# Row loads with six tokens per partition, loads on two queues, a 64-column local mask and a new opening list, in a sparse-attention and gated-MLP kernel

## The chip, the cores and the metric

The kernel runs on one core of a Trainium2 chip. TensorE (PE) multiplies; VectorE (DVE), ScalarE (ACT) and GpSimd (POOL) do the elementwise work; SyncE (SP) only issues transfers (DMAs), and ACT issues some too. The metric is the device time of one execution in microseconds.

## The reference

Eight batches, eight heads, 576 tokens, 64 values per head, all in float32. Heads 0 to 3 see the last 32 tokens (local), heads 4 to 7 see every 32nd token before them (strided). The result, with heads side by side (512 wide), goes through a gated MLP whose gate mixes tokens.

```python
scores = scale * np.matmul(q, k.transpose(0, 1, 3, 2))
rel = pos[:, None] - pos[None, :]
mask_local = (rel >= 0) & (rel < 32)
mask_strided = (rel >= 0) & (pos[None, :] % 32 == pos[:, None] % 32)
attn = softmax(where(mask, scores, -1e9)); x = attn @ v     # heads h < 4 local, others strided

h = gelu_tanh(x @ w_in)                  # w_in 512 x 1024
u, v = h[..., :512], h[..., 512:]
v_n = (v - mean(v)) / sqrt(var(v) + 1e-6) * g_ln
v_s = einsum('ts,bsd->btd', w_sg, v_n) + b_sg[None, :, None]    # 576 x 576 over tokens
return x + (u * v_s) @ w_out             # w_out 512 x 512
```

The weights w_in and w_out arrive as 64-bit floats and are turned into pairs of float32r values (high and remainder) on the core.

## The kernel before

The work is cut into short *steps*, each a two- or three-letter name with an argument; three lists give the order in which they are emitted: START for batch 0 (with batch 1's attention beside it), CYCLE for batches 1 to 6 and LAST for batch 7. A `-` behind a name means batch 0's own attention, `+` the batch after the next, nothing the next batch (for attention) or the present one (for the MLP). Each engine runs its instructions in the order of the list, so a list sets the order on five engines and on the DMA queues at once. A `^` chooses the other of two ways for that step, such as DVE in place of POOL.

The heads go in pairs `hh` = 0 to 3: 0 and 1 are local, 2 and 3 strided. For each pair and batch:

- `LP` (`qk_rows`, batches 0 and 1) loads q and k with tokens on partitions; `TP` and `TC` (`qk_turn`, `qk_turned`) transpose them on PE and copy them from PSUM with ACT. `LQ` and `TQ` do this for the later batches with loads of 32-token blocks and DVE transposes. `TZ` and `LZ` set zeros, `LV` (`v_load`) loads v.
- `SL` and `SS` are the local and strided scores on PE; `MK`, `MX`, `SB`, `EX`, `SU`, `ML` are the softmax: mask added, maximum, subtraction, exponential, sum, scaling. `SB` and `ML` run on POOL, or on DVE with `^`.
- `PL`, `CL`, `CM` and `PS`, `CS` transpose the probabilities, `VA` (`VX`, `VY`) and `PV`, `PW` multiply with v; `XH` and `XL` split the result into high part and remainder (`xt`), `XR` and `XD` store it to memory for the final addition.

The MLP: `va` to `vd` and `v` (products with the v half of w_in), `g` (gelu), `ls`, `lr`, `lm`, `lh`, `ll` (layer norm; `lr` computes the reciprocal root by a seed and three Newton steps, on POOL or with `^` on DVE), `u` and `ug`, `s` (the mixing over tokens, with w_sg transposed by `wl`, `wt`, `wh`, `wm`), `sm`, `sh`, `sl` (gate and its split), `o`, `o2`, `os`, `od` (the output product, the addition of x, the store), `r` and `rt` (x read back).

The conversion of the 64-bit weights is done once, in sixteen parts (0 to 7 of w_in, v half first; 8 to 15 of w_out): `cl` loads, `ca`, `cc` (DVE) and `cb`, `cd` (ACT) take the bits apart, `ce` adds the low word (DVE, or ACT and POOL with `^`), `cf` multiplies (POOL, or DVE with `^`), `cg` (ACT) writes the high part, `ch` (POOL, or DVE with `^`) the remainder. The buffer `stage` holds five parts of w_in, `ob` two of w_out.

All loads are issued by SP (`sp.dma_start`), the stores by ACT. The local mask `mask_l` is 128 x 8 x 64: eight equal blocks, of which two differ in 32 rows, where the first 32 keys lie before the first token.

Of the kernel before, what the change touches and what calls it, by code (L numbers as in the profile page):

```python
# [8 lines left out]
F32 = mybir.dt.float32  # L9
# [15 lines left out]
mk= cl=:1 cl=:2 wb= wc= wd= ca=:1 cb=:1 cc=:1 TZ-:0 LP-:0 TP-:1 ca=:2 cl=:0 ca=:0 cb=:0 cc=:0  # L25
TP-:0 TC-:0 cb=:2 cc=:2 mp= LP-:1 TP-:2 TC-:2 cd=:1 ce=:1 TC-:1 cl=:3 ca=:3 LZ-:0 cd=:0 LP-:3
TZ-:1 TP-^:3 TC-:3 SL-^:0 ml= LP-:2 we= cb=:3 MK-:4 cc=:3 MX-:4 TP-^:6 SB-:4 SL-:1 MK-:5 TP-:4
cd=:3 ce=:3 cf=^:3 TP-^:5 mr= TP-:7 cl=:8 MX-:5 ca=:8 cf=^:1 ce=^:0 SB-^:5 cd=:2 cf=:0 TC-:6
TC-:7 cg=:3 cl=:9 ca=:9 cb=:8 cc=:8 cg=:0 SS-^:3 MK-:3 TC-:5 ce=^:2 LP:1 EX-:4 SU-:4 LP:0 cb=:9
EX-:5 SU-:5 cc=:9 ML-^:4 TP:2 TC-:4 TZ:1 TP^:0 TC:0 cl=:6 cg=:1 ch=:3 SS-^:2 cf=:2 cd=:9 cg=:2  # L30
PL-:4 ch=^:1 ML-^:5 cd=:8 TC:2 LZ-:1 ce=^:8 TP^:3 TC:3 LV-:0 CL-:4 TP:1 ca=:6 ce=:9 cb=:6 MK-:2
MX-:2 cf=:9 cg=:9 SB-^:2 PL-:5 CL-:5 ch=:9 wl=:1 wt=^:1 wh=:1 MX-:3 SB-:3 ch=:2 ch=:0 cc=:6
EX-:2 VX-:0 XHa-:0 cl=:5 wm=:1 ca=:5 cb=:5 CM-:5 VY-:0 TZ:0 TC:1 SU-:2 cd=:6 XLa-:0 LV-:1 XR-:0
EX-:3 SU-:3 cl=:13 ca=:13 VA-:1 XH-:1 XL-:1 cl=:7 XR-:1 XHb-:0 cb=:13 ca=:7 cf=:8 ce=:6 LP:3
ML-:2 PS-^:2 LV-:2 CS-:2 cc=:13 cb=:7 ML-:3 PS-^:3 CS-:3 cc=:5 cd=:5 cf=^:6 LV-:3 SL^:0 cl=:4
SL^:1 MK:0 MX:0 cd=:13 XD-:0 XD-:1 PV-:3 PW-:3 cc=:7 ca=:4 SB^:0 cb=:4 PV-^:2 PW-:2 cc=:4 va:0
XH-:2 XL-:2 XH-:3 XL-:3 XLb-:0 XR-:2 xt vb:0 vc:0 vd:0 ce=^:13 EX:0 LP:2 cd=:4 g:0 ce=^:4 lg=
va:1 cf=:4 vb:1 XD-:2 ce=:5 SU:0 ML^:0 vc:1 LZ:1 vd:1 XR-:3 XD-:3 cf=^:5 TP^:4 v:2 ls:0 lr:0
lm:0 cd=:7 cg=:4 ce=:7 cf=^:7 cg=:6 ch=:6 g:1 ls:1 TP:7 TC:4 vh wl=:4 wt=:4 TC:7 TP^:6 cf=^:13
TC:6 cg=:7 wl=:0 wt=^:0 lm:1 vl SS:3 wh=:0 wm=:0 wh=:4 cg=:5 TP:5 wl=:2 wt=^:2 TC:5 wm=:4 ch=:4  # L40
MK:3 cl=:15 ch=^:5 cg=:8 ch=:7 ch=^:8 SS:2 MK:2 MX:2 lh:0 u:1 g:2 ug:1 lr:1 lh:1 ll:0 wh=:2 u^:2
ls:2 ca=:15 cb=:15 cc=:15 cl=:10 ca=:10 ll:1 lm:2 wm=:2 wl=:3 wt=^:3 wh=:3 TZ+:0 wo= wm=:3
# [59 lines left out]
def tile_sparse_attention_moe(  # L102
# [63 lines left out]
    mask_l = cpool.tile([P, 8, 64], F32, name="mask_l")  # L166
# [10 lines left out]
    def local_mask():  # L177

        pool.memset(mask_l, 0.0)
        for g in range(4):  # L180
            r = slice(32 * g, 32 * g + 32)
            pool.affine_select(
                out=mask_l[r], in_=mask_l[r], pattern=[[0, 8], [1, 64]],
                compare_op=ALU.is_gt, fill=NEG, base=0, channel_multiplier=-1,
            )
            pool.affine_select(
                out=mask_l[r], in_=mask_l[r], pattern=[[0, 8], [-1, 64]],
                compare_op=ALU.is_ge, fill=NEG, base=32, channel_multiplier=1,
            )

        for g, blk in ((0, 1), (1, 5)):
            pool.memset(mask_l[32 * g : 32 * g + 32, blk, 0:32], NEG)
# [158 lines left out]
    def sg_load(t):  # L351
        n = P if t < KF else TL
        wsg_st[t] = p2.tile([P, S], F32, tag="gt", name=f"wsg_{t}")
        sp.dma_start(wsg_st[t][:n], w_sg[t * P : t * P + n, :])
# [52 lines left out]
    def qk_load(b, hh):  # L407

        for nm, src in (("q", q), ("k", k)):
            raw = p1.tile([P, NB, 32], F32, tag="raw", name=f"raw{nm}_{b}_{hh}", bufs=4)  # L410
            for hp in range(2):
                for dh in range(2):
                    qd = 32 * (2 * hp + dh)
                    sp.dma_start(
                        raw[qd : qd + 32],
                        src[b, 2 * hh + hp, :, 32 * dh : 32 * dh + 32].rearrange(
                            "(n t) d -> t n d", t=32
                        ),
                    )
            state[b, hh, "raw" + nm] = raw  # L420
# [19 lines left out]

    def qk_rows(b, hh):

        for nm, src in (("q", q), ("k", k)):
            raw = p1.tile([P, KF + 1, 2, D], F32, tag="raw", name=f"row{nm}_{b}_{hh}", bufs=4)
            for hp in range(2):
                rows = src[b, 2 * hh + hp]
                sp.dma_start(
                    raw[:, 0:KF, hp], rows[0 : KF * P].rearrange("(c p) d -> p c d", p=P)
                )
                sp.dma_start(raw[:TL, KF, hp], rows[KF * P : S])  # L450
            state[b, hh, "row" + nm] = raw
# [12 lines left out]

    def qk_turned(b, x):
        hh, nm = x // 2, "qk"[x % 2]
# [6 lines left out]
        src = state[b, hh, "turn" + nm][:, 0:S]  # L473
        if hh >= NH // 2:
            dst = dst.rearrange("p (c t) -> p c t", c=NCL)
            src = src.rearrange("p (t c) -> p c t", c=NCL)
        act.copy(dst, src)
# [5 lines left out]
    def v_load(b, hh):  # L483
        if hh < NH // 2:
            vv = state[b, hh, "v"].rearrange("p h (j d) -> p h j d", d=D)
            for hp in range(2):
                src = v[b, 2 * hh + hp]
                sp.dma_start(vv[0:64, hp], src.rearrange("(j p) d -> p j d", p=64))
                sp.dma_start(
                    vv[64:128, hp, 1:NJ, :],  # L490
                    src[32 : S - 32].rearrange("(j p) d -> p j d", p=64),
                )
                sp.dma_start(vv[96:128, hp, 0, :], src[0:32])
        else:
            vt = state[b, hh, "v"] = p2.tile([P, 2, NJ * D], F32, tag="v", name=f"v_{b}_{hh}")
            for hp in range(2):
                src = v[b, 2 * hh + hp].rearrange("(p n r) d -> n p (r d)", n=2, r=8)
                for n in range(2):
                    sp.dma_start(vt[TP * n : TP * n + TP, hp, 0 : 8 * D], src[n])
# [30 lines left out]
    def strided_scores(b, hh):  # L530
        qT, kT = state[b, hh, "q"], state[b, hh, "k"]
        ps = state[b, "s", hh] = at_tile(f"ss_{b}_{hh}")
        for rb in range(8):
            for n in range(2):
                c = 8 * n + rb
                for hp in range(2):
# [3 lines left out]
                        qT[hr, c * TP : c * TP + TP],  # L540
                        kT[hr, c * TP : c * TP + TP],
# [6 lines left out]
    def sm_mask(b, x):  # L548

        if x in PARTS:  # L550
# [3 lines left out]
            for a in range(2):  # L554
                if x != 5 - a:
                    m = mask_l[:, 4 * a : 4 * a + 4].rearrange("p a b -> p (a b)")
                    dve.tensor_tensor(
                        sm[:, 512 * a : 512 * a + 512].rearrange("p (h w) -> p h w", h=2),
                        ps[:, :, 256 * a : 256 * a + 256],
                        m[:, None, :].to_broadcast([P, 2, 256]), op=ALU.add,  # L560
                    )
            if x != 4:
                pr = state[b, "sr"]
                dve.tensor_tensor(
                    sm[:, 1024:1152], pr[:, 0, 0:128],
                    mask_l[:, 2:4].rearrange("p a b -> p (a b)"), op=ALU.add,
# [241 lines left out]
    def ln_rsqrt(b, i):  # L808
# [235 lines left out]
```

## Time and profile before

| | |
|---|---|
| Median of 3 runs | 591.0 us (590.96 to 591.58) |
| Profiled execution, its own time | 590.0 us |
| Span from first to last instruction | 588.0 us |
| Mean granted TensorE clock | 0.991 |
| PE, busy | 550.4 us (94%) |
| DVE, busy | 398.1 us (68%) |
| ACT, busy | 270.5 us (46%) |
| POOL, busy | 199.7 us (34%) |
| Data moved by DMA | 69.95 MB, 119 GB/s over the span |

Shares are of the span. PE's busy time counts the matrix products; the weight loads that overlap them stand apart as PEld. A stretch's DMA share is the mean busy share of the 16 DMA engines. Issuing a DMA isn't counted as busy time, on SP or on ACT; it shows as a row of that engine's queue (SPq, ACTq). All steps are recorded in one helper, so every row has the same line number, and tiles tell them apart: `stage` and `cv` belong to the conversion, `rowq` and `rowk` to the row loads, `turnq` and `turnk` to their transposes, `sa`/`sr` and `ss` to local and strided scores, `sml` and `sms` to their softmax.

### The profile page before, as it was taken

How to read it: one execution, taken by the hardware profiler on the slowest of the kernel's cores; microseconds unless marked ns; L12 is line 12 of the kernel's file. 1: busy time of each engine (PE TensorE's matmuls, PEld its weight loads, DVE VectorE, ACT ScalarE, POOL GpSimd, SP SyncE). 2: the span in 40 equal slices, each digit the busy share in tenths (PEclk: the TensorE clock that was granted, in tenths of full speed). 3: DMA queues.
4: the chain of work that ended last, by engine and by line, in shares of the span. 5: the costliest groups of instructions: out<-in, count | busy, mean ns of one | idle time of the engine just before them, and what ended most of it. 6: DMA issues, size and time to landing. Idle time of an engine off the chain costs nothing.

```text
span 588.0 us, 15066 instructions
## 1 busy us (share of the span) xinstructions
PE 550.4 (94%) x6113; PEld 489.9 (83%) x6113; DVE 398.1 (68%) x665; ACT 270.5 (46%) x397; POOL 199.7 (34%) x471
## 2 busy tenths in 40 slices
PE   1766899999999999999999999999999999999996
PEld 1555678888999889988998889988998889988995
DVE  2879997776884577756775577756875588545532
ACT  2486575741573327542572328442572338433320
POOL 6334187240542027220642026310732035302310
PEclk9996999999999999999999999999999999999999
DMA  6778764477842689248832678248831781056002
GB/s 185 178 175 195 151 166 86 104 170 172 181 66 57 146 165 164 41 102 162 168 63 59 159 142 160 42 113 166 169 61 53 166 168 37 1 118 156 1 2 89
DMA packets 262630, 69.95 MB, mean 119 GB/s; under 512 B 248289, under 2 KB 248289, under 8 KB 262562
## 3 DMA queue, kind: packets, MB, share of 16 engines
q1 hardware_dynamic: 181538, 50.12, 39.4%
q10 hardware_dynamic: 81024, 18.89, 15.8%
q8 instruction: 48, 0.79, 0.6%
q14 instruction: 20, 0.16, 0.1%
HBM read 50.09 MB, written 18.87 MB: 117 GB/s over the span
## 4 chain that ended last, share of the span: by engine, by line
PE 77%; DVE 8%; POOL 4%; DMA 3%; ACT 3%; issue 3%; SPq 1%; ACTq 0%; DVEq 0%; POOLq 0%
PE sg L83 18%; PE o L83 17%; PE v L83 15%; PE u L83 14%; PE os L83 3%; PE ss L83 2%; PE ol L83 2%; POOL nt L83 2%; PE sa L83 2%; PE pts L83 2%; DMA stage<-in_moe_w_in_dram 1%; DMA rowq<-in_q_dram 1%; DVE sr L83 1%; PE ptl L83 1%; SPq L83 1%
## 5 line engine op out<-in xcount | busy, mean ns | idle before, releaser
L83 PE MATMUL sg<-wsh,vg 128*128 128x288 f32 x512 | 112.8, 296 | 0.0
L83 PE MATMUL u<-xt,wih 128*128 128x288 f32 x512 | 103.5, 297 | 1.1 <-ACT u L83 1.0
L83 PE MATMUL o<-woh,vg 128*128 128x512 f32 x288 | 95.7, 398 | 1.1 <-DVE gt L83 1.1
L83 PEld LDWEIGHTS sg<-wsh,vg 128*128 128x128 f32 x512 | 85.5, 188 | 0.3
L83 PE MATMUL v<-wih,xt 128*128 128x512 f32 x256 | 83.4, 397 | 1.5 <-ACT xt L83 0.9
L83 PEld LDWEIGHTS u<-xt,wih 128*128 128x128 f32 x512 | 82.1, 188 | 2.6 <-ACT u L83 1.8
L83 PE MATMUL u<-xt,wil 128*128 128x288 f32 x256 | 75.6, 295 | 0.4 <-DVE wil L83 0.4
L83 PE MATMUL sg<-wsl,vg 128*128 128x288 f32 x256 | 75.3, 294 | 0.0
L83 ACT ACT_TABLE_LOAD x40 | 51.3, 1283 | 51.5 <-DMA xd<-xs 26.9
L83 PEld LDWEIGHTS o<-woh,vg 128*128 128x128 f32 x288 | 54.1, 188 | 12.5 <-issue 1.3
L83 PEld LDWEIGHTS v<-wih,xt 128*128 128x128 f32 x256 | 48.0, 188 | 13.3 <-ACT xt L83 1.3
L83 PE MATMUL o<-wol,vg 128*128 128x512 f32 x144 | 56.3, 391 | 0.0
L83 DVE TENSOR_TENSOR ob<-o,xn 128x512 f32<-128x512 f32 x32 | 22.0, 691 | 46.5 <-PE o L83 40.7
L83 ACT CAST vg<-gt 128x576 fp32r<-128x576 f32 (+2 forms) x48 | 22.9, 509 | 61.1 <-DVE gt L83 61.1
L83 PE MATMUL v<-wil,xt 128*128 128x512 f32 x128 | 50.1, 391 | 0.0
L83 PEld LDWEIGHTS u<-xt,wil 128*128 128x128 f32 x256 | 48.0, 188 | 0.6 <-DVE wil L83 0.6
L83 PEld LDWEIGHTS sg<-wsl,vg 128*128 128x128 f32 x256 | 48.2, 188 | 0.0
L83 DVE BATCH_NORM_STATS2 bnst<-hv 128x6 f32<-128x512 f32 (+1 forms) x40 | 27.0, 676 | 17.4 <-ACT hv L83 17.4
L83 POOL TENSOR_TENSOR sms<-sms,sr 100x576 f32<-100x576 f32 x14 | 16.2, 1158 | 64.6 <-DVE sr L83 63.4
L83 DVE TENSOR_TENSOR gt<-sg,u 128x576 f32<-128x576 f32 x32 | 23.6, 739 | 21.3 <-PE sg L83 12.5
L83 ACT ACTIVATE u<-u 128x576 f32<-128x576 f32 x32 | 20.9, 652 | 28.6 <-PE u L83 28.4
L83 POOL TENSOR_SCALAR va<-mv 128x2 f32<-128x2 f32 (+1 forms) x23 | 8.3, 363 | 70.1 <-DVE mv L83 68.9
(152 smaller groups left out, 1094.6 us busy)
## 6 DMA issues: line engine op xcount, KB each, us to landing
xd<-xs ACTq DMA_DIRECT2D x128, 72.0 KB
xn<-xd SPq DMA_DIRECT2D x8, 1024.0 KB
out_dram<-ob ACTq DMA_DIRECT2D x32, 256.0 KB
rawq<-in_q_dram SPq DMA_DIRECT2D x96, 72.0 KB
rawk<-in_k_dram SPq DMA_DIRECT2D x96, 72.0 KB
v<-in_v_dram SPq DMA_DIRECT2D x32, 144.0 KB
v<-in_v_dram SPq DMA_DIRECT2D x64, 72.0 KB
stage<-in_moe_w_in_dram SPq DMA_DIRECT2D x8, 512.0 KB
```

The source lines that it names most:

```text
L83: ins = self.tc.keep_in_program_order(op(*args, **kwargs))
```

## The change

- `START` is written anew. It has the same 428 steps as before, in another order, and with `^` on other steps.
- `loads()` stands in for `sp` in `cl`, `wl`, `LP`, `LQ` and `LV`: with `^` the load is issued by ACT. In CYCLE and LAST no load carries `^`.
- `qk_rows` puts six consecutive tokens on each of 96 partitions, one transfer per head and tensor; before, tokens went over 128 partitions in four blocks and a fifth of 64, in two transfers. The six transposes of 96 partitions yield token order `c, t` (token 6t + c), and the copy behind them, in steps, puts the tokens in their natural order, for strided heads too. The strided scores of batches 0 and 1 then read q and k with 16 words between elements; later batches keep theirs class by class.
- `v_load` joins transfers of two heads: 5 instead of 6 for a local pair, 2 instead of 4 for a strided one.
- `mask_l` is 128 x 64 and is broadcast in the addition; the rows before the first token are set by a `memset` on the sum, one for each half of the heads.
- On DVE the Newton step of `lr` is three instructions instead of four.

The first words of the two lists:

```
before: mk= cl=:1 cl=:2 wb= wc= wd= ca=:1 cb=:1 cc=:1 TZ-:0 LP-:0 TP-:1 ca=:2 cl=:0 ca=:0 cb=:0 cc=:0
        TP-:0 TC-:0 cb=:2 cc=:2 mp= LP-:1 TP-:2 TC-:2 cd=:1 ce=:1 TC-:1 cl=:3 ca=:3 LZ-:0 cd=:0 LP-:3 ...
after:  mk= mp= cl=:3 ca=:3 cl=:1 LP-^:3 cb=:3 cc=:3 ca=:1 cb=:1 cl=:0 cc=:1 cd=:1 cd=:3 cl=:2 TZ-:0
        ca=:2 cl=:8 ml= ce=:3 ca=:0 cb=:0 ce=^:1 TP-^:6 TC-:6 cb=:2 TP-^:7 TC-:7 cf=^:1 cg=:1 cc=:2 ...
```

```diff
+    def loads():
+        return act if alt[0] else sp
...
-    mask_l = cpool.tile([P, 8, 64], F32, name="mask_l")
+    mask_l = cpool.tile([P, 64], F32, name="mask_l")
...
-        sp.dma_start(conv[i], halves[i][0])
+        loads().dma_start(conv[i], halves[i][0])
...
+    RP = 96
+    RT = S // RP
...
-            raw = p1.tile([P, KF + 1, 2, D], F32, tag="raw", name=f"row{nm}_{b}_{hh}", bufs=4)
+            raw = p1.tile([P, RT, 2, D], F32, tag="raw", name=f"row{nm}_{b}_{hh}", bufs=4)
             for hp in range(2):
-                rows = src[b, 2 * hh + hp]
-                sp.dma_start(
-                    raw[:, 0:KF, hp], rows[0 : KF * P].rearrange("(c p) d -> p c d", p=P)
+                loads().dma_start(
+                    raw[0:RP, :, hp], src[b, 2 * hh + hp].rearrange("(p c) d -> p c d", c=RT)
                 )
-                sp.dma_start(raw[:TL, KF, hp], rows[KF * P : S])
...
+        for c in range(RT):
             pe.transpose(
-                ps[:, kk * P : kk * P + n],
-                raw[:n, kk].rearrange("p h d -> p (h d)"), ident[:n, :n],
+                ps[:, c // 3, c % 3 * RP : c % 3 * RP + RP],
+                raw[0:RP, c].rearrange("p h d -> p (h d)"), ident[0:RP, 0:RP],
             )
...
-        act.copy(dst, src)
+        act.copy(
+            dst.rearrange("p (t a c) -> p t a c", a=2, c=RT // 2),
+            state[b, hh, "turn" + nm][:, :, 0:SH].rearrange("p a (c t) -> p t a c", t=RP),
+        )
...
-                sp.dma_start(vv[96:128, hp, 0, :], src[0:32])
+            loads().dma_start(vv[96:128, :, 0, :], src[:, 0:32].rearrange("h p d -> p h d"))
...
+            src = v[b, 2 * hh : 2 * hh + 2].rearrange("h (p n r) d -> n p h (r d)", n=2, r=8)
+            for n in range(2):
+                loads().dma_start(vt[TP * n : TP * n + TP, :, 0 : 8 * D], src[n])
...
+        if by_rows(b):
+            qc, kc = (x[:, 0:S].rearrange("p (t c) -> p c t", c=NCL) for x in (qT, kT))
+        else:
+            qc, kc = (x[:, 0:S].rearrange("p (c t) -> p c t", c=NCL) for x in (qT, kT))
...
-                        qT[hr, c * TP : c * TP + TP],
-                        kT[hr, c * TP : c * TP + TP],
+                        qc[hr, c],
+                        kc[hr, c],
...
+                        half.rearrange("p h (g w) -> p h g w", w=64),
+                        ps[:, :, 256 * a : 256 * a + 256].rearrange("p h (g w) -> p h g w", w=64),
+                        mask_l[:, None, None, :].to_broadcast([P, 2, 4, 64]), op=ALU.add,
                     )
+                    dve.memset(half[32 * a : 32 * a + 32, :, 64:96], NEG)
...
+            if eng is dve:
+                dve.scalar_tensor_tensor(t[c], t[c], -0.5, va[c], op0=ALU.mult, op1=ALU.mult)
+                dve.scalar_tensor_tensor(y[c], t[c], 1.5, y[c], op0=ALU.add, op1=ALU.mult)
+                continue
```

More of the change, by code (lines that the diff above doesn't have):

```diff
@@ L31 @@
[L31 to L42, printed above, removed]
@@ new lines @@
+sh:3 cb=:12 ML^:3 LZ:0 cg=:10 cc=:12 VA^:1 cd=:12 LQ+:3 sm:0 ch=:8 cg=:15 cl=:14 ch=^:10 ca=:14
+ch=^:15 ce=^:12 cf=:12 sh:0 sl^:0 TQ+:0 cg=:12 LV:0 sm:1 sh:1 sl:1 r cb=:14 cc=:14 EX:2 LQ+:1
+VA:0 XR:1 PS:3 CS:3 o:0 o^:1 ch=:12 sl:3 cd=:14 ce=:14 cf=^:14 cg=:14 SU:2 ML^:2 XH:0 XL:0
+ch=:14 XH:1 XL:1 LV:3 o^:2 o^:3 o2:2 os:2 XD:1 XR:0 XD:0 o2:0 o2:3 os:3 LV:2 PS^:2 o2:1 PV:3
+PW:3 CS:2 od:2 PV:2 od:3 PW:2 TQ+:1 XH:3 LZ+:1 XL:3 XH:2 XR:3 XD:3 os:1 XR:2 XD:2 od:1 LZ+:0
+os:0 od:0 LV+^:0 LQ+:2 LV+:1 XL:2
@@ L182, in local_mask @@
             pool.affine_select(
-                out=mask_l[r], in_=mask_l[r], pattern=[[0, 8], [1, 64]],
+                out=mask_l[r], in_=mask_l[r], pattern=[[1, 64]],
                 compare_op=ALU.is_gt, fill=NEG, base=0, channel_multiplier=-1,
@@ L186, in local_mask @@
             pool.affine_select(
-                out=mask_l[r], in_=mask_l[r], pattern=[[0, 8], [-1, 64]],
+                out=mask_l[r], in_=mask_l[r], pattern=[[-1, 64]],
                 compare_op=ALU.is_ge, fill=NEG, base=32, channel_multiplier=1,
             )
-        for g, blk in ((0, 1), (1, 5)):
-            pool.memset(mask_l[32 * g : 32 * g + 32, blk, 0:32], NEG)
     mask_s = cpool.tile([P, TP], F32, name="mask_s")
@@ L353, in sg_load @@
         wsg_st[t] = p2.tile([P, S], F32, tag="gt", name=f"wsg_{t}")
-        sp.dma_start(wsg_st[t][:n], w_sg[t * P : t * P + n, :])
+        loads().dma_start(wsg_st[t][:n], w_sg[t * P : t * P + n, :])
     def sg_transpose(t):
@@ L456, in qk_turn @@
         raw = state[b, hh, "row" + nm]
-        ps = state[b, hh, "turn" + nm] = mm_tile(f"turn{nm}_{b}_{hh}").rearrange("p a c -> p (a c)")
-        for kk in range(KF + 1):
-            n = P if kk < KF else TL
+        ps = state[b, hh, "turn" + nm] = mm_tile(f"turn{nm}_{b}_{hh}")
+        for c in range(RT):
             pe.transpose(
-                ps[:, kk * P : kk * P + n],
-                raw[:n, kk].rearrange("p h d -> p (h d)"), ident[:n, :n],
+                ps[:, c // 3, c % 3 * RP : c % 3 * RP + RP],
+                raw[0:RP, c].rearrange("p h d -> p (h d)"), ident[0:RP, 0:RP],
             )
@@ L485, in v_load @@
             vv = state[b, hh, "v"].rearrange("p h (j d) -> p h j d", d=D)
+            src = v[b, 2 * hh : 2 * hh + 2]
             for hp in range(2):
-                src = v[b, 2 * hh + hp]
-                sp.dma_start(vv[0:64, hp], src.rearrange("(j p) d -> p j d", p=64))
-                sp.dma_start(
+                loads().dma_start(vv[0:64, hp], src[hp].rearrange("(j p) d -> p j d", p=64))
+                loads().dma_start(
                     vv[64:128, hp, 1:NJ, :],
-                    src[32 : S - 32].rearrange("(j p) d -> p j d", p=64),
+                    src[hp, 32 : S - 32].rearrange("(j p) d -> p j d", p=64),
                 )
-                sp.dma_start(vv[96:128, hp, 0, :], src[0:32])
+            loads().dma_start(vv[96:128, :, 0, :], src[:, 0:32].rearrange("h p d -> p h d"))
         else:
             vt = state[b, hh, "v"] = p2.tile([P, 2, NJ * D], F32, tag="v", name=f"v_{b}_{hh}")
[L496 to L499, printed above, removed]
+            src = v[b, 2 * hh : 2 * hh + 2].rearrange("h (p n r) d -> n p h (r d)", n=2, r=8)
+            for n in range(2):
+                loads().dma_start(vt[TP * n : TP * n + TP, :, 0 : 8 * D], src[n])
     def blk_pos(hh, hp, j):
@@ L555, in sm_mask @@
                 if x != 5 - a:
[L556 removed]
+                    half = sm[:, 512 * a : 512 * a + 512].rearrange("p (h w) -> p h w", h=2)
                     dve.tensor_tensor(
[L558 to L560 removed]
+                        half.rearrange("p h (g w) -> p h g w", w=64),
+                        ps[:, :, 256 * a : 256 * a + 256].rearrange("p h (g w) -> p h g w", w=64),
+                        mask_l[:, None, None, :].to_broadcast([P, 2, 4, 64]), op=ALU.add,
                     )
+                    dve.memset(half[32 * a : 32 * a + 32, :, 64:96], NEG)
             if x != 4:
@@ L564, in sm_mask @@
                 dve.tensor_tensor(
-                    sm[:, 1024:1152], pr[:, 0, 0:128],
-                    mask_l[:, 2:4].rearrange("p a b -> p (a b)"), op=ALU.add,
+                    sm[:, 1024:1152].rearrange("p (g w) -> p g w", w=64),
+                    pr[:, 0, 0:128].rearrange("p (g w) -> p g w", w=64),
+                    mask_l[:, None, :].to_broadcast([P, 2, 64]), op=ALU.add,
                 )
```

44 lines of the change are left out of this document (24 added, 20 removed).

## The prediction

> **What bounds the kernel now.** I read the busy time of each engine by stretches of the span first, then the chain of work that ended last, then the order of time of the SP queue, and only then single tiles. The columns of the first view are: stretch, its length, busy time (and instructions) of PE, PEld, DVE, ACT and POOL, granted TensorE clock, share of the DMA engines, GB/s.
>
> ```profile
> 0.00:10.00 10.00, 0.00 (x0) 0.00 (x0) 3.41 (x4) 2.87 (x4) 8.53 (x27) 1.00 0.60 164
> 10.00:20.00 10.00, 7.11 (x93) 4.96 (x94) 5.83 (x16) 5.41 (x9) 1.47 (x4) 1.00 0.89 220
> 20.00:30.00 10.00, 7.12 (x92) 5.04 (x92) 7.07 (x14) 2.96 (x6) 4.81 (x8) 1.00 0.65 160
> 30.00:40.00 10.00, 8.21 (x151) 6.86 (x151) 7.36 (x15) 7.91 (x17) 3.78 (x5) 1.00 0.66 155
> 40.00:50.00 10.00, 4.79 (x50) 3.32 (x48) 9.47 (x10) 5.95 (x12) 6.95 (x8) 0.73 1.05 203
> 50.00:62.00 12.00, 9.00 (x255) 7.99 (x257) 11.76 (x27) 7.85 (x14) 2.36 (x3) 0.80 0.82 208
> 62.00:100.00 38.00, 34.38 (x325) 28.61 (x320) 33.01 (x60) 22.87 (x44) 24.39 (x55) 1.00 0.63 135
> 100.00:140.00 40.00, 37.46 (x343) 33.70 (x341) 29.42 (x53) 20.81 (x37) 13.71 (x17) 1.00 0.59 135
> 140.00:584.00 444.00, 442.30 (x4819) 399.46 (x4818) 290.60 (x472) 193.81 (x257) 133.73 (x347) 1.00 0.52 107
> ```
>
> From 140 to 584 us PE idles 1.7 us of 444. From 62 to 140 it idles 6.2 of 78. Before 62 it idles 25.8 of 62. So nearly everything that can be won lies before the first v product, and what follows it is a solid run of PE to the end:
>
> ```profile
> 62.32 0.50 PE L83 MATMUL v<-wih,xt 128*128 128x512 f32 x1
> ...
> 583.50 0.69 DVE ob L83
> ```
>
> The first row is from PE's order of time, the last from the end of the chain: the addition that waits for the last product. From 62.3 to 583.5 are 521.2 us. The products in it are the same after the change, so the time is the moment of the first v product plus that run, corrected for what PE has done ahead of it and for waits behind it.
>
> Ahead of 62 us DVE is the engine that is full, but only late: 21.2 busy of the 22 us from 40 to 62, against 23.7 of the first 40. Why it is short of work there is told by its waits (what waited, for whom: total, times, longest) and by the SP queue:
>
> ```profile
> DVE cv L83 <- DMA stage<-in_moe_w_in_dram: 9.3, 3, 5.1
> DVE cv L83 <- ACT cv L83: 2.2, 2, 1.4
> DVE cx L83 <- DMA cs<-in_moe_w_out_dram: 2.0, 1, 2.0
> ```
>
> ```profile
> 4.29 2.17 SPq L83 DMA_DIRECT2D rowq<-in_q_dram  x4
> 6.50 2.34 SPq L83 DMA_DIRECT2D rowk<-in_k_dram  x4
> 8.88 0.58 SPq L83 DMA_DIRECT2D stage<-in_moe_w_in_dram  x1
> ...
> 33.48 2.28 SPq L83 DMA_DIRECT2D rowk<-in_k_dram  x4
> 35.86 0.53 SPq L83 DMA_DIRECT2D stage<-in_moe_w_in_dram  x1
> 36.43 4.06 SPq L83 DMA_DIRECT2D v<-in_v_dram  x6
> ```
>
> SP issues without a pause: from 4.29 to 36.43 us it sends 48 row loads and five loads of weights, 0.61 us each. DMA engines are at 0.65 to 0.66 of their time from 20 to 40 us, so there the issuing is the limit and not the moving. Of every pair of row loads one carries only 16 KB and costs an issue like the 128 KB one (four in 2.17 to 2.34 us).
>
> **The change, part by part.** *Row loads.* One step LP issues 4 transfers instead of 8, in b = 0 and 1 only; v loads go from 6 to 5 and from 4 to 2. Counting the steps of both lists up to the first v product gives 97 issues before (89 on SP, 8 on ACT) and 60 after (42 on SP, 18 on ACT). At 0.61 us, SP's share of that falls from 54 to 26 us, and 18 issues on ACT take 11 us where 8 took 5. The bytes remain: counted over the lists, 10.6 MB before the first v product and 10.1 after. The DMA engines' share above sums to 48.3 us of full work up to 62 us, so even with free issue the first v product can't come before some 46 us (48.3 x 10.1 / 10.6). That caps the gain of this part at 16 us. What I book is the DVE waits for loads that are not the first one: 9.3 + 2.0 - 5.1 = 6.2 us. DVE's waits for ACT (2.2 in the row above) I leave as they are, since the list has as many such hand-overs as before.
>
> *Six transposes of 96 in place of four of 128 and one of 64.* The columns moved are equal (576).
>
> ```profile
> 10.35 1.41 PE L83 MATMUL turnk<-ident,rowk 128*128 128x128 f32 x5 [10.35 <-DMA rowk<-in_k_dram]
> 78.23 0.86 PE L83 MATMUL turnk<-ident,rowk 128*128 128x128 f32 x5
> L83 PE MATMUL ss<-kT,qT x256: 199/199/273, 30.0 to 85.7; 64*36 64x36 f32 x128
> 81.25 1.31 PE L83 MATMUL ss<-kT,qT 64*36 64x36 f32 x64
> L83 ACT COPY qT<-turnq x8: 617/629/644, 14.2 to 80.2; 128x576 f32<-128x576 f32 x8
> ```
>
> Between no cost and 6/5 of the 1.41 us (0.28 each) or of the later 0.86 us (0.17 each), 16 turns cost 0 to 3.6 us; PE idles around most of them, I book 0.5. The copy behind each turn now reads PSUM in steps; half of the copies in the row above (the strided heads) did so before, and shortest and longest differ by 27 ns, so nothing is booked.
>
> *Strided scores of b = 0 and 1* read q and k from SBUF with 16 words between elements instead of one after the other. No row of this trace has PE reading SBUF so. Bounds: nothing, as for the ACT copies, and a doubling, 1.31 us more for each of four steps (64 matmuls each), 5.2 us, or the 6.7 us of all 256 by their 199 to 273 ns if they overlap as now. I take nothing for the forecast (the copies are the nearest row of a stepped read) and keep the doubling as a rival.
>
> *Local mask.*
>
> ```profile
> L83 POOL TENSOR_SCALAR_AFFINE_SELECT mask_l<-mask_l x8: 648/695/1007, 5.1 to 10.6; 32x512 f32<-32x512 f32 x8
> L83 DVE TENSOR_TENSOR sml<-sa,mask_l x16: 678/688/693, 20.0 to 470.8; 128x512 f32<-128x512 f32 x16
> L83 DVE TENSOR_SCALAR cv<-stage x8: 383/424/879, 5.1 to 63.0; 128x512 int32<-128x512 int32 x8
> L83 POOL TENSOR_SCALAR_AFFINE_SELECT mask_s<-mask_s 36x36 f32<-36x36 f32 x2 | 0.4, 210 | 0.1
> ```
>
> Eight selects of 512 columns become eight of 64, near the 210 ns of the 36-column one: POOL falls from 5.8 to 1.7 us. POOL isn't on the path there, but while it runs them DVE's first field extractions take up to 879 ns instead of 424. I book no gain, as DVE then waited for a load. The mask addition stays at 688 ns, 512 elements either way. Two DVE memsets per batch are new, some 0.2 us each by the nearest small rows (the 210 ns select, the 175 ns in the next fence). Four of the sixteen fall before the first v product (0.8 us, within the list's sum below); the twelve others lie where DVE is busy 290.6 of 444 us, so they cost nothing; without that cover, 2.4 us.
>
> *The list.* Both lists hold the same 428 steps, differently ordered and differently dealt out. POOL gets less; DVE gets the seed-and-Newton step of one v tile (eleven small instructions), two more gate remainders and one more subtraction, and gives up one scaling.
>
> ```profile
> L83 DVE TENSOR_SCALAR sr<-sr 100x16 f32<-100x16 f32 x4 | 0.7, 175 | 0.1
> L83 DVE TENSOR_TENSOR vg<-gt,vg 128x576 fp32r<-128x576 f32 x1 | 0.7, 747 | 0.0
> 32.23 1.52 DVE L83 TENSOR_TENSOR sms<-ss,mask_s 36x576 f32<-36x576 f32 x2 [0.53 <-PE ss L83]
> ...
> 45.70 3.77 DVE L83 TENSOR_SCALAR stage<-stage 128x512 int32<-128x512 int32 x1
> 46.64 2.48 POOL L83 TENSOR_TENSOR wil<-cv,wih 128x512 fp32r<-128x512 f32 x2
> ```
>
> That is 11 x 0.175 + 2 x 0.75, some 3.4 us more DVE over the list. Added up to the step where as much of PE's work is done as at the first sg product before, the list sum on DVE is 82.1 us after against 80.4 before, so I book 1.7 us as a loss. On the other side, head pair 3 comes first. The first weights reach DVE 5.1 us after the start (the longest wait above); its rows are issued right behind them, and two turns of 1.4 us, their copies of 0.6 and the scores of some 2 follow, so that even with 4 us in the queues DVE can mask them by 15 to 16 us. Before, the first strided scores were masked at 32.23. This is work for DVE in just the stretch where it waited, and the reason why I book all 6.2 us. The 3.77 us instruction takes 0.42 elsewhere (the 424 ns row, same shape); it ended within half a microsecond of POOL's work beside it. I price what becomes of it from -3.3 (it does not recur) to +3.3 (one more of it) and take -1.6, half of it away, because POOL has some 10 us less to do in the list.
>
> Sum: -6.2 - 1.6 + 1.7 + 0.5 = -5.6 us. The profiled execution took 590.0 us (span 588.0, 2.0 around it), so it becomes 584.4; the median of the runs shown is 591.0, 1.0 above, so the median becomes 585.4.
>
> **The rivals.** (1) *Deeper.* If DVE really runs full from its first load on, the waits for ACT shrink by half too (1.1), the 3.77 us stall goes whole (1.7 more), and PE does another 2 us of later work ahead of v: 585.4 - 4.8 = 580.6. For it speaks the size of the idle time (17.1 us of DVE before 62); against it that a chain DVE, ACT, DVE, ACT stands behind every half of the weights.
>
> (2) *It changes nothing.* The moving, not the issuing, is the bound: share 1.05 and 0.82 after 40 us, and all bytes still have to come by the first v product. Then what is issued early lands late, the 6.2 us stay, and 591 remains, within a microsecond. Against it: 0.65 and 0.66 from 20 to 40. [...]
>
> (3) *Slower: the second queue blocks ACT.* When ACT and SP issued together the issues took longer, and the activation behind them waited:
>
> ```profile
> 59.67 5.23 ACTq L83 DMA_DIRECT2D xd<-xs  x6
> 61.88 2.28 SPq L83 DMA_DIRECT2D rowq<-in_q_dram  x3
> 64.95 0.72 ACT L83 ACTIVATE cv<-cv,ebias 128x512 int32<-128x512 int32 x1 [5.22 <-DMA xd<-xs]
> ```
>
> 0.87 us each on ACT. Ten issues more there ahead of the first v product cost ACT 8.7 us; behind them in its queue stand the exponent and mantissa steps that DVE waits for. If all of it passes on to DVE: 585.4 + 8.7 = 594.1. It decides from 0.56 us per extra issue passed on in full (5.6 in all). Against it: ACT is busy 32.9 of the first 62 us and can give way.
>
> (4) *Stepped reads slow PE.* Doubled strided scores cost 5.2 us; b = 0's two steps fall where PE idles, b = 1's in the full run, so half of it counts: 588.0. [...]
>
> **How the numbers follow.** Forecast 0.50, deeper 0.20, nothing 0.09, ACT blocked 0.14, stepped reads 0.07. The forecast's own range is 582 to 589. The range for 8 in 10 goes from 578.5, which holds most of the deeper case, to 591.0, which leaves out the blocked queue and half of the unchanged case. A measurement of this kernel can tell 0.2%, 1.2 us: faster is below 589.8 (forecast, deeper and stepped reads, less 0.01 that goes to slower), the same up to 592.2.
>
> **What would show it.** First v product near 56 us instead of 62.3, with the run behind it still 521 us, within 3. DVE's waits for stage loads near 5 us, its first one. SP pausing before 36 us. Transposes of 96 rows at or below 0.3 us apart, strided scores still 1.3 us per 64. The prediction is wrong if the first v product comes early but the gain is given back before 140 us (DVE then is the cause, and its busy time from 62 to 100 would be near 38), if ACT's waits for its own DMA issues rise by 5 us or more, or if PE's time after 140 us changes at all.

## The result and the profile after

The changed kernel takes 581.07 us (median of 5 runs, 580.32 to 583.45) where the kernel before takes 591.58 on the same chip (590.96 to 592.88): ratio 0.9826, interval 0.981 to 0.9842, a gain of 10.5 us. Measured once more beside other kernels on another chip it was 581.43 against 591.89, ratio 0.9829 (0.9802 to 0.9856). Each of the two measurements left a profile: the first was of an execution of 583.45 us, its slowest, the second of one of 580.09. Where they differ I give both.

The moment of the first v product, from PE's order of time, first profile and then second (62.32 before):

```profile
55.70 0.48 PE L83 MATMUL v<-wih,xt 128*128 128x512 f32 x1
```

```profile
54.11 0.48 PE L83 MATMUL v<-wih,xt 128*128 128x512 f32 x1
```

From there to the last product of PE are 521.4 and 519.7 us (521.1 before). So in the first profile the difference to before (590.0 - 583.45 = 6.55) is the shift of the first v product (6.62) and nothing else; in the second (9.9) it is 8.2 of shift and 1.4 behind it.

That the run behind the first v product keeps its length is a sum of changes that nearly cancel. Its first 77.7 us and the rest up to the last product of PE, before and then in the first profile (columns as in the prediction: PE, PEld, DVE, ACT, POOL, granted clock, DMA share, GB/s):

```profile
62.32:140.00 77.68, 71.52 (x656) 62.07 (x653) 62.11 (x111) 43.68 (x80) 38.10 (x71) 1.00 0.61 135
140.00:583.46 443.46, 442.30 (x4819) 399.46 (x4818) 290.10 (x471) 193.81 (x257) 133.73 (x347) 1.00 0.52 107
```

```profile
55.70:133.38 77.68, 75.91 (x839) 67.30 (x838) 67.37 (x132) 44.81 (x84) 30.59 (x52) 1.00 0.68 143
133.38:577.14 443.76, 440.12 (x4672) 396.59 (x4671) 290.12 (x478) 193.46 (x257) 134.94 (x347) 1.00 0.52 107
```

PE idles 4.4 us less in the first stretch (6.2, now 1.8) and 2.5 us more in the second (1.2, now 3.6), and it is busy 2.2 us longer in the two together. In the second profile these are 4.8, 1.5 and 1.8 us.

The stretches of the first profile:

```profile
0.00:10.00 10.00, 0.00 (x0) 0.00 (x0) 4.80 (x13) 2.95 (x5) 4.53 (x25) 1.00 0.77 252
10.00:20.00 10.00, 6.18 (x86) 5.58 (x87) 5.72 (x11) 7.14 (x12) 2.34 (x3) 1.00 0.96 195
20.00:30.00 10.00, 7.33 (x167) 6.10 (x165) 7.33 (x15) 5.03 (x9) 3.04 (x6) 1.00 0.82 215
30.00:40.00 10.00, 6.70 (x91) 5.82 (x91) 9.59 (x19) 7.58 (x16) 7.71 (x12) 0.96 1.03 175
40.00:50.00 10.00, 8.64 (x139) 7.35 (x141) 9.48 (x19) 7.57 (x15) 5.44 (x8) 0.50 0.72 183
...
56.00:94.00 38.00, 37.47 (x366) 33.05 (x365) 35.35 (x76) 27.04 (x52) 21.84 (x38) 1.00 0.74 154
...
134.00:578.00 444.00, 439.51 (x4670) 396.11 (x4668) 290.26 (x478) 193.46 (x257) 134.94 (x347) 1.00 0.52 107
```

DVE is full from 30 us on, where before it was full from 40. The DMA engines, at 0.60 to 0.66 in three of the first four stretches before, are at 0.77 to 1.03: they now move data most of the time. DVE's waits up to 62 us, and SP's queue in the order of time, both from the first profile:

```profile
DVE cv L83 <- ACT cv L83: 3.5, 3, 1.9
DVE pat L83 <- POOL pat L83: 3.3, 1, 3.3
DVE cv L83 <- POOL stage L83: 2.5, 1, 2.5
...
DVE cv L83 <- DMA stage<-in_moe_w_in_dram: 0.9, 1, 0.9
```

```profile
0.79 1.95 SPq L83 DMA_DIRECT2D stage<-in_moe_w_in_dram  x4
5.06 0.33 SPq L83 DMA_DIRECT2D cs<-in_moe_w_out_dram  x1
6.57 3.75 SPq L83 DMA_DIRECT2D rowq<-in_q_dram  x2
12.32 1.80 SPq L83 DMA_DIRECT2D rowk<-in_k_dram  x2
...
22.06 0.35 SPq L83 DMA_DIRECT2D wsg<-in_moe_w_sg_dram  x1
26.28 1.25 SPq L83 DMA_DIRECT2D rowq<-in_q_dram  x2
```

The waits for loads (9.3 + 2.0 before) are down to 0.9, and SP, which issued without a pause up to 36 us, now pauses several times (for 3.9 us from 22.4 on). New are a wait for POOL's mask pattern at the very start, which the first load hid before, and one for POOL's share of the first weight part.

DVE is busy or idle up to the first v product, so that moment is a sum of two numbers. The row of the stretch up to it, for before and for the two profiles of the changed kernel:

```profile
0.00:62.32 62.32, 36.55 (x643) 28.41 (x643) 45.22 (x83) 32.96 (x60) 27.89 (x53) 0.92 0.78 185
```

```profile
0.00:55.70 55.70, 34.17 (x622) 29.78 (x623) 40.74 (x83) 32.16 (x57) 24.56 (x53) 0.88 0.84 195
```

```profile
0.00:54.11 54.11, 30.50 (x622) 26.45 (x623) 40.75 (x83) 32.29 (x57) 24.94 (x53) 0.84 0.88 201
```

Before: 45.2 busy and 17.1 idle. After: 40.7 busy and 15.0 (13.4) idle. The change took 4.5 us from DVE's work ahead of that point and 2.1 to 3.7 us from its idle time. Such a sum can be made for every engine; DVE is the one to read because it is full in the last stretch ahead of that point. The same two numbers sort the experiments below. Their profiles are of single executions, which can lie several us from the median.

### The profile page after: what moved, and what is told of

The parts are those of the page before. It is cut to its first block, busy times and chain, and to the rows that moved or that the text cites. A ratio compares the mean times of both kernels' runs of the same rounds, so it can differ in the third digit from the quotient of the medians.

```text
span 581.7 us, 14975 instructions
## 1 busy us (share of the span) xinstructions
PE 550.2 (95%) x6129; PEld 493.7 (85%) x6129; DVE 398.9 (69%) x692; ACT 270.4 (46%) x396; POOL 190.1 (33%) x452
## 3 DMA queue, kind: packets, MB, share of 16 engines
q10 hardware_dynamic: 89024, 22.88, 18.6%
## 4 chain that ended last, share of the span: by engine, by line
PE 64%; DVE 11%; POOL 7%; ACT 5%; DMA 5%; issue 5%; ACTq 2%; SPq 0%; DVEq 0%; POOLq 0%
PE sg L83 18%; PE o L83 15%; PE v L83 11%; PE u L83 7%; POOL nt L83 4%; PE os L83 3%; PE ol L83 3%; ACTq L83 2%; POOL y L83 2%; PE pts L83 2%; DMA rowk<-in_k_dram 2%; PE sa L83 2%; DVE sr L83 1%; ACT L83 1%; ACT vg L83 1%
## 5 line engine op out<-in xcount | busy, mean ns | idle before, releaser
L83 ACT CAST vg<-gt 128x576 fp32r<-128x576 f32 (+2 forms) x48 | 22.8, 509 | 61.1 <-DVE gt L83 61.1
L83 DVE SCALAR_TENSOR_TENSOR vg<-hv,y,vg 128x512 fp32r<-128x512 f32 x32 | 23.0, 761 | 15.7 <-ACT vg L83 15.7
L83 PEld LDWEIGHTS o<-wol,vg 128*128 128x128 f32 x144 | 27.1, 188 | 4.9
```

What stands on the lines that cost most here:

```text
L83: ins = self.tc.keep_in_program_order(op(*args, **kwargs))
```

## The experiments

Ratios are to the kernel before, run on the same chip beside them.

**1. The old list under the new loads.** All of the change but its first list: START as before.

```diff
-START = """ mk= mp= cl=:3 ca=:3 cl=:1 LP-^:3 ...
+START = """ mk= cl=:1 cl=:2 wb= wc= wd= ...
```

> The changed kernel with the opening list of before (no load on ACT). Theory A (the gain comes from fewer issues and from the order that the list makes of them, together): halving the row loads alone takes about 24 issues of 0.56 us out of SP's queue before the first v product, DVE's waits for stage loads fall from 9.3 to some 7 us, the stepped reads cost up to 2.5 us: 588 to 590, first v product at 59 to 61 us. Theory B (the list carries it all): no gain is left and the stepped reads show, 591 to 594. Theory C (the parts carry it): 581 to 584.

585.75 us, ratio 0.9901 (0.987 to 0.9932): 5.4 us of the 10.5. That lies between theories A (588 to 590) and C (581 to 584). The first v product came at 59.43 us, of which DVE was busy 43.7 and idle 15.8: 1.5 us less work and 1.3 us less idle time than before. Of the work, 1.1 us is one instruction, the stretched extraction, which took 2.64 us here in place of 3.77. (DVE's waits for stage loads still were 8.9 us in this profile: the idle time that went is mostly not those waits.)

**2. All loads on one queue.**

```diff
-        return act if alt[0] else sp
+        return sp
```

> The changed kernel with every load issued by SP, same list. [...] Rival (two queues issue side by side): the ten loads taken off ACT cost SP 6 us before the first v product, 584 to 587.

584.12 us, ratio 0.9877 (0.9849 to 0.9905), 3 us slower than with two queues, as the rival has it. DVE's waits for stage loads were 7.3 us again in place of 0.9, its work up to the first v product (58.57) 39.8 us as with two queues. The second queue is worth 3 us, and it is the smaller part. (The two intervals just touch.)

**3. The old row loads under the new list.** `qk_rows`, `qk_turn` and `qk_turned` as before (eight transfers a step, issued by SP or ACT as the list says), with the list, the v loads and the mask of the change. The scores read q and k one element after the other.

> The changed kernel with the row loads of before (eight transfers for each step, 128 tokens on partitions, five transposes, strided scores reading one element after the other). Theory A: 24 issues more before the first v product, 12 to 14 us of issuing of which a half shows at the first v product, against 2 us saved by the unstepped reads: 584 to 588. Rival (issuing is no limit under the new list): the saved reads alone show, 578 to 580.

591.33 us, ratio 0.9995 (0.9968 to 1.0021): no gain at all, which neither theory had. First v product at 59.45 us, DVE busy 39.5 and idle 20.0. The list does cut DVE's work ahead of v (by 5.7 us), but with twice the transfers DVE idles 2.9 us more than before. This profile is of an execution of 588.16 us, 3 us below the median, and the run behind its first v product took 522.2; where the other 3 us lie it can't show.

**4. Strided scores read without steps.** Batches 0 and 1 take their columns one after the other. This kernel leaves out the right choice of tokens: count and shapes of the products stay, but they multiply other tokens than they should.

```diff
-        if by_rows(b):
+        if False:
```

> The changed kernel with the strided scores of batches 0 and 1 reading q and k one element after the other (they then multiply the wrong tokens; the count and shapes of instructions stay). If the stepped read costs what the trace shows, 64 matmuls take 1.3 to 1.4 us again where they took 2.3 in batch 1, and the end comes 1.9 to 2.7 us earlier: 578.4 to 579.2. Rival (the steps lie beside DVE's work and PE only waits longer): 580.5 to 581.5.

580.9 us, ratio 0.9815 (0.9788 to 0.9842): no difference to the changed kernel. But the step itself did get faster. PE's order of time, first with the stepped reads (the changed kernel's first profile), then without:

```profile
16.21 2.35 PE L83 MATMUL ss<-kT,qT 64*36 64x36 f32 x64 [0.73 <-ACT kT L83]
...
72.18 2.29 PE L83 MATMUL ss<-kT,qT 64*36 64x36 f32 x64
```

```profile
15.97 2.14 PE L83 MATMUL ss<-kT,qT 64*36 64x36 f32 x64 [0.73 <-ACT kT L83]
...
70.68 1.31 PE L83 MATMUL ss<-kT,qT 64*36 64x36 f32 x64
```

Later than 60 us a stepped step costs 0.98 us more; near 16 us only 0.2. There are two of the dear ones, 1.9 us of PE. From the first v product to the first sg product, changed kernel (second profile) and this one:

```profile
54.11:92.15 38.04, 37.52 (x368) 33.12 (x367) 35.48 (x75) 27.21 (x53) 22.23 (x38) 1.00 0.73 154
```

```profile
54.02:92.60 38.58, 35.98 (x368) 31.05 (x365) 35.86 (x76) 27.09 (x53) 20.39 (x38) 1.00 0.73 152
```

PE is busy 1.5 us less and the stretch is no shorter: PE waits instead, while DVE has 35.5 and 35.9 us of work in it. The slower reads lie beside that.

**5. The changed kernel once more**, as the base for 6 to 8; its numbers stand in the first section.

> The changed kernel itself once more, for a second trace beside the ones with one thing undone. Every trace so far has 520.4 to 522.2 us from the first v product to the last product, whatever was changed ahead of it. Theory A (the moment of the first v product is all that differs): an execution of 581 us shows it at 53 to 54 us, not at the 55.7 of the first trace. Rival (something after 140 us differs from run to run): first v product at 55 to 56 again, and a shorter run behind it.

The execution of 580.09 us had its first v product at 54.11 and a run behind it 1.7 us shorter than the first profile's (519.7 against 521.4). So each theory holds in part: the moment of the first v product is half of the 3.4 us between these two executions, and the run behind it the other half.

**6. New row layout, eight transfers.** Each of the four transfers of a step is cut in two, of three tokens per partition each. Bytes, tiles, transposes and list are those of the change.

```diff
-                loads().dma_start(
-                    raw[0:RP, :, hp], src[b, 2 * hh + hp].rearrange("(p c) d -> p c d", c=RT)
-                )
+                rows = src[b, 2 * hh + hp].rearrange("(p c) d -> p c d", c=RT)
+                for c0 in (0, 3):
+                    loads().dma_start(raw[0:RP, c0 : c0 + 3, hp], rows[:, c0 : c0 + 3])
```

> The changed kernel with the same row loads, layout and bytes, but each head's six tokens in two transfers of three: eight issues for each step again. Theory A (the number of issues is what counts): most of the gain goes, 587 to 591, as with the row loads of before (591.3). Rival (the layout counts: 96 partitions, whole rows of 1536 bytes): 581 to 583.

590.45 us, ratio 0.9968 (0.9948 to 0.9989). This is the plainest run of the study: nothing but the count (and with it the size) of the row transfers differs from the changed kernel, and 9 of the 10.5 us are gone by the medians, 8 by the ratios. First v product at 58.76, DVE busy 39.8, idle 18.9. Up to there the DMA engines were at 0.78, less than in the changed kernel (0.84 and 0.88), so they had room, and the moving is not what got dearer. At the start both queues issue eight row loads and four weight loads together (SP's queue, then ACT's):

```profile
0.79 7.10 SPq L83 DMA_DIRECT2D stage<-in_moe_w_in_dram  x4
```

```profile
3.09 4.49 ACTq L83 DMA_DIRECT2D rowk<-in_k_dram  x4
7.63 0.72 ACT L83 ACTIVATE cv<-cv,ebias 128x512 int32<-128x512 int32 x1 [5.33 <-DMA stage<-in_moe_w_in_dram]
```

The four weight loads that took SP 1.95 us to issue take 7.10, and ACT's first activation stands behind ACT's own issues until 7.63 (5.76 in the changed kernel; the load named in brackets is not what it waited for last). DVE's longest wait stands later, for a weight load that SP issued at 25.29 us (18.27 in the changed kernel), behind a pause of 7.2 us in SP's queue:

```profile
25.29 0.35 SPq L83 DMA_DIRECT2D stage<-in_moe_w_in_dram  x1
30.27 0.43 DVE L83 TENSOR_SCALAR cv<-stage 128x512 int32<-128x512 int32 x1 [4.63 <-DMA stage<-in_moe_w_in_dram]
```

What held SP back in that pause no run isolates. So the count of transfers is shown to be the cause of the loss, and issuing time to be a part of the way there; that it is all of it is not shown.

The loss does not all lie ahead of the first v product. From there to PE's last product, the changed kernel's two profiles and then this run:

```profile
55.70:577.14 521.44, 516.04 (x5510) 463.89 (x5508) 357.49 (x609) 238.27 (x341) 165.53 (x399) 1.00 0.54 112
```

```profile
54.11:573.78 519.67, 515.66 (x5510) 464.02 (x5508) 356.98 (x609) 238.52 (x341) 165.79 (x399) 1.00 0.54 113
```

```profile
58.76:588.25 529.49, 520.33 (x5510) 467.82 (x5508) 358.31 (x610) 238.23 (x340) 164.60 (x399) 0.99 0.54 111
```

This profile is of an execution of 594.70 us, the slowest of twelve. Behind the first v product it is 8 to 10 us longer: PE idles 9.2 us in place of 5.4 and 4.0 (3.1 of it for v loads, 2.5 for u), and takes 4.3 to 4.7 us more for the same 5510 products, with the granted clock at 0.50 for some 6 us behind one of these waits and 3.4 us behind another. Late loads cost twice here, then. How the 9 us of the median divide, one profile can't tell.

**7. Half as many again.** One transfer for both heads: two a step.

```diff
-            for hp in range(2):
-                loads().dma_start(
-                    raw[0:RP, :, hp], src[b, 2 * hh + hp].rearrange("(p c) d -> p c d", c=RT)
-                )
+            loads().dma_start(
+                raw[0:RP],
+                src[b, 2 * hh : 2 * hh + 2].rearrange("h (p c) d -> p c h d", c=RT),
+            )
```

> The changed kernel with both heads of a pair in one transfer: two issues for each step instead of four, the same bytes in the same places. Theory A (issues are still the limit ahead of the first v product): 16 issues fewer there, 9 us of issuing, of which a third shows: 576 to 579. Rival (issuing no longer limits, the moving and DVE do): 580 to 582.

583.51 us, ratio 0.9873 (0.9845 to 0.99): not better but about 2 us worse, with intervals that just touch; neither theory had that. In the profile, of the slowest of its six executions (586.73), the first v product came at 56.21, DVE was idle 15.7 us ahead of it, and the run behind it took 523.7. Fewer issues brought nothing more. The DMA engines' share between 10 and 20 us was 1.06, and single issues took long although few were made:

```profile
5.51 3.03 SPq L83 DMA_DIRECT2D rowk<-in_k_dram  x1
```

The edit changes one thing beside the count: a transfer now takes 64 values of one head and 64 of the other in turn, where the changed kernel's takes six tokens of one head on end. That the larger transfers come in a less suitable order is my reading; no run isolates it, nor that turn.

**8. The small mask alone, on the kernel before.**

> The kernel before with the small local mask alone (eight selects of 64 columns on POOL, two memsets on DVE for each batch). Theory A (POOL is off the path there, and DVE waits for a load behind it): no change, 590 to 592. Rival (DVE's slow first instructions beside POOL's selects set the pace): 588 to 589.5.

591.24 us, ratio 0.9996 (0.9981 to 1.0012): nothing. (In its profile the first v product came 1.9 us later, at 64.3, and the run behind it took 520.2, 0.9 us less: part of a shift of that moment in a single profile can be given back.) What it does is make room: the row tiles of six tokens are 128 words larger per partition in each of four buffers (2 KB), the mask is 1.75 KB smaller.

**9 to 11. Two attempts to gain more.** After 130 us the changed kernel's PE waits once for u, up to 156.9 us in the first profile (1.8 us) and up to 154.3 in the second (1.4), which before did not occur; ACT stands there behind POOL's reciprocal root. Run 9 moves that root to DVE; run 10 moves the first weight part's addition (DVE's 2.5 us wait for POOL) to DVE; run 11 does both.

```diff
 CYCLE: -lr:1 EX:0 lr:0    +lr^:1 EX:0 lr^:0      (9, 11)
 START: -ce=^:1            +ce=:1                 (10, 11)
```

> The changed kernel with lr:1 and lr:0 of the list CYCLE taken by DVE in place of POOL. In the changed kernel PE waits once more after 140 us, 1.4 to 2.4 us for the tile u at 154 to 157 us, where ACT stood 3.3 to 3.6 us waiting for POOL's reciprocal root; before the change that wait isn't there. Theory A (the chain on POOL is what is late now that the first v product comes 7 us earlier): that wait goes, and the time falls by 1 to 2 us against the changed kernel, to 579 to 580.5. Theory B (DVE is as full there, and takes the small instructions only behind its own work): the wait stays or another takes its place, 581 to 583.

> The changed kernel with the addition of the first weight part's low word (ce:1) on DVE in place of ACT and POOL. DVE waits 2.5 us for that tile at 12 to 15 us. Theory A (what DVE waits for early is worth its length at the first v product): the first v product comes 1 to 2.5 us earlier, 579 to 580.4. Theory B (DVE is short of loads there and the waits behind it grow by as much; the DMA engines are near their full share up to 40 us): no change, 580.4 to 582.

> Both of these edits. If each of them removes a wait on the path, the gains add up, 577.5 to 579.5; if neither does, 580.5 to 583.

Run 9: 604.9 us, ratio 1.0235 (1.0217 to 1.0252), some 24 us slower than the changed kernel (by the two ratios), which neither theory had. The wait at u went, and a dearer one came in each of six batches (PE's waits after 140 us, DVE's order of time, and three stretches around one of them):

```profile
PE ss L83 <- DVE kT L83: 18.4, 6, 3.6
```

```profile
217.90 0.15 DVE L83 TENSOR_SCALAR va<-mv 128x2 f32<-128x2 f32 x1
...
221.90 0.16 DVE L83 SCALAR_TENSOR_TENSOR y<-nt,y 128x2 f32<-128x2 f32 x1
222.08 1.20 DVE L83 STREAM_TRANSPOSE qT<-rawq 128x576 f32<-128x576 f32 x1
223.14 1.16 DVE L83 STREAM_TRANSPOSE kT<-rawk 128x576 f32<-128x576 f32 x1
```

```profile
221.40:224.50 3.10, 0.14 (x4) 0.08 (x5) 2.98 (x7) 2.89 (x4) 0.00 (x0) 1.00 1.23 121
...
225.20:228.60 3.40, 3.40 (x98) 3.33 (x93) 3.33 (x7) 0.28 (x1) 1.97 (x4) 0.50 0.78 103
```

22 small instructions of 0.2 us stand on DVE ahead of the transposes that the strided scores need, so the scores come 3 us late, and in five of the six cases the clock is then at 0.50 for some 3.4 us. The run behind the first v product is 542.4 us, 21 us longer than in the first profile of the changed kernel and 23 longer than in the second: 15.5 to 17 us of PE's idle time (the six waits, 18.4, less the old one and smaller ones) and 5.4 to 5.8 us more busy time for the same products, some 1.1 us for each stretch at 0.50. The first v product, at 56.69, came 1.0 and 2.6 us later. PE's pause ahead of the stretch shown was 2.96 us. Pauses of 1.9 us in run 10 (24 products of u behind it took 4.99 us, 3.45 in later batches) and of 2.3 us in run 6 (32 of `os` behind it took 2.19 us, 1.22 before it) were also followed by such a stretch, and the one of 1.8 us in the changed kernel's first profile was not (the clock reads 1.00 from 156.9 to 165 us). What brings the stretch on, no run isolates.

Run 10: 583.03 us, ratio 0.9862 (0.9848 to 0.9875). The first v product came at 53.68 us, earlier than in both profiles of the changed kernel, and yet the time is some 2 us longer, with intervals that just touch: behind it the run was 522.5 us, with a wait of 1.9 us for u at 153 us and a half-speed stretch behind that. Neither theory had it. Run 11: 603.43, ratio 1.0211 (1.0185 to 1.0237), as 9, and far from both of its expectations, with the first v product at 53.35.

**12. Eight transfers on one queue**, runs 2 and 6 together.

> Eight row transfers a step as in the kernel with split rows, and all loads on SP. With split rows and two queues ACT's first activation started at 7.63 us behind eight issues of its own (5.76 in the changed kernel), and DVE's later weight loads waited 4.6 us. Theory A (what costs is the number of issues that have to be made, wherever they are made): one queue makes it worse, 592 to 597 against 590.5. Theory B (what costs is that ACT's activations stand behind its own issues): one queue is better, 585 to 588, and ACT's first activation starts by 6 us again.

592.43 us, ratio 1.0008 (0.9992 to 1.0024), as theory A has it. ACT's first activation did start at 5.76 us again, and it didn't help: DVE's waits for stage loads were 8.3 us, and the first v product came at 60.13. With runs 2 and 6 this closes a square:

| | four transfers a step | eight |
|---|---|---|
| loads on SP and ACT | 0.9826, 0.9829 | 0.9968 |
| loads on SP alone | 0.9877 | 1.0008 |

Halving the transfers is worth 8 us with either, the second queue 2 to 3 us with either. The first is far outside the intervals; those of one and two queues just touch with four transfers and are apart with eight.

## Why the prediction was right, and where its sizes were off

It forecast 585.4 (578.5 to 591.0); 581.07 came. Direction and place were right: the gain lies ahead of the first v product, and the run behind it stays within 1.5 us of 521, if only as a sum of changes. The size was 5.6 booked against 10.5. What came is nearest in number to the rival *deeper* (580.6), but not by its mechanism: DVE's waits for ACT's `cv`, which it halves, rose from 2.2 to 3.5 us (3.2), the run behind v, which it shortens by 2 us, is 1.4 us shorter in one profile and not in the other, and only its stall came in large part. The two large errors had opposite signs: idle time was booked at -6.2 and fell by 2.1 to 3.7, work was booked at about nothing (1.7 - 1.6) and fell by 4.5. That the sum came as near as it did is in part luck. By its own steps:

- *DVE's waits for later loads, -6.2.* The waits for loads went even further than that (11.3 to 0.9), so the row was read rightly; but DVE's idle time up to the first v product fell by only 2.1 to 3.7 us, because other waits came: for POOL's pattern 3.3, where the first load had stood, for POOL's part of the addition 2.5, for ACT 1.3 more. Booking a wait at its full length was the error, and it was on the generous side.
- *The list, +1.7 of DVE work.* This step failed, with the wrong sign. DVE's work ahead of the first v product fell by 4.5 us, and in runs 2, 3, 6 and 12, which share the list and not the loads, it was 39.5 to 40.1 too, against 43.7 under the old list (run 1). The prediction added up the list to the point where as much of PE's work is done as at the first *sg* product, and took that for the first *v* product. From the first v to the first sg product, before and in the first profile:

```profile
62.32:101.12 38.80, 35.18 (x324) 29.49 (x321) 33.78 (x62) 23.99 (x45) 24.98 (x56) 1.00 0.61 131
```

```profile
55.70:93.79 38.09, 37.56 (x369) 33.12 (x367) 35.45 (x75) 27.13 (x53) 21.84 (x38) 1.00 0.74 155
```

  The new list puts 1.7 us more of DVE's work between the two. With the stall below (2.5) that is all but 0.4 of the 4.5. At the first sg product itself DVE's work is down too, from 79.0 to 76.2 us, and by 0.4 without the stall, so the 1.7 us of loss came at neither point. The strided scores of head pair 3 did reach DVE early, at 18.6 us (32.2 before), some 3 us later than worked out.
- *The stall of 3.77 us, -1.6.* It is part of those 4.5. The longest stretched extraction is now this one, 0.9 us over the 0.42 of its kind:

```profile
39.82 1.32 DVE L83 TENSOR_SCALAR cv<-stage 128x512 int32<-128x512 int32 x1
```

  So 2.5 us went (3.35 to 0.90) where half of it was booked. With it the sum for the first profile is -2.1 (idle) - 2.5 (stall) - 2.0 (list) = -6.6, and -8.2 with the second's idle time: the shift of the first v product.
- *Transposes, +0.5.* Six of 96 cost less, not more (five of 128 took 1.41 early and 0.86 later):

```profile
14.29 1.19 PE L83 MATMUL turnk<-ident,rowk 96*128 96x96 f32 x6 [0.65 <-DMA rowk<-in_k_dram]
...
69.71 0.66 PE L83 MATMUL turnk<-ident,rowk 96*128 96x96 f32 x6
```

- *Stepped reads, 0.* The time was right by luck, and the reason wrong. The prediction took the ACT copies for the nearest row and expected 1.3 us per 64; it is 2.3. The rival's doubling, an estimate, was nearer: run 4 shows 1.75 times in batch 1. The reads with 64 bytes between elements cost 0.98 us per 64 products there and 0.2 near 16 us; run 4 also shows that the 1.9 us of batch 1 lie beside DVE's work.
- *Mask, 0.* Right (run 8). The eight selects take 0.23 us each, the addition stays as it was, and a memset is 0.11 us (the tile mask_l and the tile sml of the changed kernel: shortest, median, longest in ns):

```profile
L83 DVE TENSOR_TENSOR sml<-sa,mask_l x16: 620/692/693, 23.6 to 463.8; 128x512 f32<-128x512 f32 x16
L83 POOL TENSOR_SCALAR_AFFINE_SELECT mask_l<-mask_l x8: 228/231/309, 3.5 to 5.5; 32x64 f32<-32x64 f32 x8
```

```profile
L83 DVE MEMSET sml<- x16: 112/112/112, 24.3 to 464.5; 32x64 f32 x16
```

- *Rival: it changes nothing, since the moving is the bound.* Runs 6 and 12 refute it under the new list: with the same bytes, count alone makes 8 us. Under the old list run 1 does, with 5.4 us. It may come true one step further on, in run 7. The second queue is worth 2 to 3 us by the square; that these are issue time alone, no run shows.
- *Rival: the second queue blocks ACT.* The mechanism is there (run 6, 1.9 us at the start), but it came with eight issues in a row; with four ACT's first activation starts as early as with none (run 12), and two queues beat one in both columns of the square.

Of the signs, the first v product near 56, the pauses of SP and the run of 521 us came; the waits for stage loads fell below the 5 foretold, the transposes stayed within 0.3 us, the 1.3 us of the scores did not hold. One sign of being wrong came too, in small: PE's time after 140 us did change, by the 2.5 (1.5) us of idle time in the second stretch above, most of them the new wait for u. The prediction had put nothing there; what hides it in the total are the 4.4 (4.8) us that PE idles less in the stretch before.

Open is where the last 2 us between single executions of the changed kernel come from. The two profiles differ in the granted clock ahead of the first v product (0.50 all through 40 to 50 us in the first, 0.67 in the second) and in DVE's idle time; no run sets the clock.

## What to carry to other kernels

Count the issues, not only the bytes: where a queue issues without a pause while the DMA engines have room (here SP up to 36 us, with the engines at 0.65 to 0.66 from 20 to 40), merge transfers, and measure every further merging by itself: halving the row transfers was worth 8 us here, halving them again, with the engines at 1.06 from 10 to 20 us, cost about 2 (run 7). A list and the loads under it are worth measuring together: here the list without the row loads gave nothing (run 3), the loads without the list half (run 1), both the whole. To book what an engine gains ahead of a fixed point, add up its busy and its idle time up to that very point; a wait that goes need not be worth its length: here 10.4 us of waits for loads went, and 2.1 to 3.7 us of idle time, as other waits stood behind them.

## What the runs showed that was not expected

- The two queues slowed each other's issues: four weight loads took SP 1.95 us to issue beside four row loads on ACT, and 7.10 us beside eight. Two queues then had these twelve issued by 7.89 us (run 6), one queue by 7.84 (run 12).
- A stepped read by PE (64 bytes between elements of 36 columns) took 2.28 to 2.35 us per 64 products in the first profile, near 16 us and later than 60 us alike, while the contiguous one went from 2.14 to 1.31 (run 4).
- In the first profile six transposes take 1.19 to 1.22 us before 31 us (twelve together 2.12) and 0.66 to 0.71 behind the first v product, although the column of the granted clock reads 1.00 in both places. In the second profile two of the early groups are fast as well (0.71 at 22.8 us). What slows the others stays open.
- A pause of PE of 3 us in a solid run cost some 4 us (run 9: 18.4 us of pauses and 5.4 to 5.8 us of longer busy time, over six), by the half-speed stretch that mostly stood behind it.
